# Half-contraction products of a GeGLU block: three stretches of them in place of four in the first and last block, and the array shape of the neighbouring attention product

## The chip, the cores and the metric

The kernel runs on one core of one Trainium2 chip. The metric is the device time of one execution in microseconds (us); a lower time is better. Engines are named as the profile names them: PE (TensorE, matrix products; PEld is its weight loading), DVE (VectorE), ACT (ScalarE), POOL (GpSimd), SP (SyncE, which here only issues transfers).

## The reference

The kernel computes a parallel transformer block on 2048 tokens of width 448, in bfloat16:

```python
xn = layernorm(x)                                  # x: 1 x 2048 x 448
q, k, v = split(xn @ wqkv)                         # 16 heads of width 28
s = where(0 <= i - j < 256, q @ k.T * 28 ** -0.5, -1e9)
attn = softmax(s) @ v @ wo
ffn = (gelu(xn @ w_gate) * (xn @ w_up)) @ w_down   # hidden width 1792, tanh gelu
out = x + attn + ffn
```

## The kernel before

**Blocks.** The tokens are worked through in four blocks of 512 columns (`QB`, `qb` 0 to 3). Each block has an attention stage and then a gate stage (`gated`, L412). During the attention stage of block n the planner (`Feed`, `share`) fills PE's time between score products with the down projection of block n-1, the q, k and v projections of block n+1 and, in block 0 and block 3, some of the up projections that the gate stage would otherwise do. After block 3 the last down projection stands alone.

**The gate stage.** The hidden width is 14 chunks of 128, taken as seven pairs f = 0, 2, ..., 12. The contraction is 448 = 3 x 128 + 64 long. So each 512-column result needs three full products (128 rows, `three`, by `mm3` at L228) and one half product (64 rows, `half`, by `mm_half` at L233). A half product uses only rows 0 to 63 or 64 to 127 of the array, so two of them, one from each side, go side by side. The last 64 rows of `w_gate` and `w_up` lie in the two sides of the tiles `wgu3` and `wug3` for that purpose. A pair f has two gate results in one tile `gt` of two accumulator banks, and two up results in single banks (`u`), unless its up half was done earlier (`early`: f = 2, 4, 8 in block 0, and 2, 4, 6, 8, 10 in block 3). An early pair holds its up results in `hT` in SBUF.

PE takes its instructions in the order in which they are written. A stretch of half products between full products is called an excursion here. L428 to L455 set it out: `dense` issues full products, `halves` half products, `end` issues the gelu on ACT (L452) and the multiplication with the up result on DVE (L454 for early pairs, L456 for others). The loop over `((0,), (2, 4), (6, 8), (10, 12))` gives four excursions in a block. Within a group of two, the first pair's full products come ahead of its halves and the second pair's full products come behind its halves, so that one excursion serves both:

```python
for fs in ((0,), (2, 4), (6, 8), (10, 12)):
    a = begin(fs[0]); dense(a, True)
    b = begin(fs[1]) if len(fs) > 1 else None
    halves(a, False)
    if b: halves(b, True)
    else: last_v()
    end(a)
    if b: dense(b, False); end(b)
```

(The quotation joins lines.) In pair 0's excursion, `last_v` puts the attention's last product with v, `pv(3)` (L552, products at L560), behind the halves. In blocks 1 to 3 these are 48 products, each on 64 rows and 32 columns of the array, in eight places; in block 0 they are 16 products on 128 rows and 32 columns. Their results are two banks `ov` (one in block 0). `add_halves` copies the first to `oc` on ACT (L548) and adds the second on DVE (L549); in block 0 one DVE copy does it (L570). In blocks 1 to 3, `pv(3)` issues this copy at once, so it stands ahead of pair 0's gelu in ACT's queue. `pv(2)`'s copy is held in the list `behind` until after the next exponential.

**Banks.** There are eight accumulator banks: two tiles of two banks for `gt` (pool `sps`, tag "s"), two single banks with tag "m" used in turn, and single banks "o" and "d". A new user of a bank waits for the engine that last read it.

**After each pair** comes `hook(f)`: the last steps of the softmax sums (`sums` at L534 to L537, `inverse` at L544, both on DVE, and `scale_o` on POOL, L527), and in blocks 0 and 1 also a normalisation of a later token tile (`norm`, L209, and in block 0 `stat`, L195 and L196, on DVE) and its transposition by a transfer that SP issues. For f = 4 it also issues the transfers of `collect`, for f = 10 those of `deliver`.

Of the kernel before, what the change touches and what calls it, by code (L numbers as in the profile page):

```python
# [16 lines left out]
P = 128  # L17
# [58 lines left out]
def kernel(  # L76
# [151 lines left out]
            nc.tensor.matmul(ps, lhsT=lhs(c), rhs=rhs(c), start=start and c == 0, stop=stop and c == 2,  # L228
                             skip_group_check=True)

    def mm_half(ps, lhs, rhs, hi, start, stop):
        p0 = 64 * hi
        nc.tensor.matmul(ps, lhsT=lhs[p0:p0 + 64], rhs=rhs[p0:p0 + 64], start=start, stop=stop,  # L233
                         tile_position=(p0, 0), skip_group_check=True)

    done = set()
    ring = [("m", "m", "d"), 0]
# [147 lines left out]
        hT = blk.tile([P, NF, QB], bf16, name="hT", tag="hT")  # L385
        hTs[qb] = hT

    def half(ps, f, gate, hi, ts, start, stop):

        w3 = wgu3 if gate != bool(hi) else wug3  # L390
        mm_half(ps, w3[:, f * P:(f + 1) * P], xnT[:, 3, ts], hi, start, stop)

    def three(ps, f, gate, ts, start, stop):
        w = wg if gate else wu
# [17 lines left out]
    def gated(qb, early, last_v, hook):  # L412

        ts = slice(qb * QB, (qb + 1) * QB)
        hT = hTs[qb]
        turn = ["o" if down_tag[0] == "d" else "d", down_tag[0]] * 4

        def begin(f):
            last_tag[0] = turn[0] if f not in early else last_tag[0]
            pr = dict(f=f, gt=phase[0].pool.tile([P, 2, QB], f32, name="gt", tag="s"), us=[])  # L420
            if f not in early:
                alone = (turn.pop(0), 1)
                tags = (("m", 2), alone)
                if qb == 0 and f == 0:
                    nxt = [ring[0][(ring[1] + i) % 3] for i in range(2)]
                    tags = [(x, 2 if x == "m" else 1) for x in nxt]
                    if "d" in nxt:
                        turn.insert(0, "o")  # L428
                for tag, n in tags:
                    pr["us"].append(psum.tile([P, QB], f32, name="u0", tag=tag, bufs=n))  # L430
            return pr

        def dense(pr, start):
            f = pr["f"]
            gs = [(pr["gt"][:, i, :], f + i, True) for i in range(2)]
            us = [(u[:, :], f + i, False) for i, u in enumerate(pr["us"])]
# [3 lines left out]
        def halves(pr, start):  # L440
            f = pr["f"]
            for i in range(2):
                if pr["us"]:
                    half(pr["gt"][:, i, :], f + i, True, 0, ts, start, not start)
                    half(pr["us"][i][:, :], f + i, False, 1, ts, start, not start)
                else:
                    half(pr["gt"][:, i, :], f + i, True, i, ts, start, not start)

        def end(pr):
            f = pr["f"]  # L450
            ge = work.tile([P, 2, QB], bf16, name="ge", bufs=2)
            nc.scalar.activation(out=ge[:, :, :], in_=pr["gt"][:, :, :], func=ACT.Gelu_apprx_tanh)  # L452
# [68 lines left out]
    def attention(qb, feeds, aux, plan):  # L521
# [25 lines left out]
        def add_halves(oc, ov):  # L547
            nc.scalar.copy(out=oc[:, :], in_=ov[0][:, :])  # L548
            nc.vector.tensor_tensor(out=oc[:, :], in0=oc[:, :], in1=ov[1][:, :], op=ALU.add)  # L549

        def pv(g):

            tags = ("o",) if not qb else ("m", "m" if g < 3 else down_tag[0])
            ov = [psum.tile([P, QB], f32, name="ov", tag=tag, bufs=2 if tag == "m" else 1) for tag in tags]
            todo = parts.pop(g)
            for n, (half, kt, q0, nq, col, p_sb) in enumerate(todo):
                k0 = 64 * half if half else 0
                r = slice(k0, k0 + (P if half is None else 64))
                for j in range(4):
                    nc.tensor.matmul(ov[half or 0][32 * j:32 * j + 32, q0:q0 + nq], lhsT=v_sb[r, kt, 4 * g + j, :],  # L560
                                     rhs=p_sb[r, j, col:col + nq], start=n == (half or 0), stop=n + len(tags) >= len(todo),
                                     tile_position=(k0, 32 * j), skip_group_check=True)
# [14 lines left out]
        for i, (scores, ncol, edges) in enumerate(steps):  # L577
            while (qb, scores[-1][0]) not in done:
                feeds[0].run()
            for fd in feeds:  # L580
                if fd.held:
                    fd.run()
            if i in pvs:
                pv(pvs[i])
            while fresh:
                apply_masks(*fresh.pop(0))
            if not qb and i - 1 in pvs:
                sums()
                inverse()
            if qb and i - 1 in pvs:  # L590
                sums()
            if qb and i - 2 in pvs:
                inverse()
            ss = phase[0].pool.tile([P, 4, QB], f32, name="sc", tag="s")
            p_sb = work.tile([P, 4, QB], bf16, name="p_sb", bufs=5)
            for g, half, kt, q0, nq, col in scores:
                k0, nk = (64 * half, 64) if half is not None else (0, P)
                for j in range(4):
                    r = slice(32 * j, 32 * j + Dh)
                    nc.tensor.matmul(ss[k0:k0 + nk, j, col:col + nq], lhsT=kT[r, g, kt * P + k0:kt * P + k0 + nk],  # L600
                                     rhs=qT[r, g, qb * QB + q0:qb * QB + q0 + nq], start=True, stop=True,
                                     tile_position=(32 * j, k0), skip_group_check=True)
                parts.setdefault(g, []).append((half, kt, q0, nq, col, p_sb))
            nc.scalar.activation(out=p_sb[:, :, 0:ncol], in_=ss[:, :, 0:ncol], func=ACT.Exp, scale=SCALE)  # L604
            while behind:
                add_halves(*behind.pop(0))
            if qb:
                fresh.append((p_sb, edges))
            else:
                for m in edges:  # L610
                    masked(p_sb, *m)
            while later:
                scale_o(*later.pop(0))
            left = len(steps) - i
            if left == 1:
                drain(feeds)
            elif not qb:
                share(feeds + [Feed()], 1e12, 0)
            else:
                to = plan.get(i, 0)  # L620
                whole = sum(f.left for f in feeds) + STEP * left + PV * sum(j > i for j in pvs)
                ahead = STEP + PV * (i + 1 in pvs) + (360 if to > 1000 else 0)
                late = 400 if i == 0 else 0
                want = (whole - late) / (left + 0.2) + late - ahead - to
                if i in pvs:
                    had = feeds[0].left
                    share(feeds[:1], min(1100, want), 0)
                    want -= had - feeds[0].left
                share(feeds, want, to)
            if aux:  # L630
                aux.pop(0)()
# [10 lines left out]
            elif copied:  # L642
                sums()

        return rest, after


    def pads(eng, dst, gs):
# [92 lines left out]
    for qb in range(NB):  # L741
# [29 lines left out]
        rest, after = attention(qb, feeds, aux, plan)  # L771
        nc.scalar.preload_act_table(ACT.Gelu_apprx_tanh)
        score_pool(2)
        if qb not in hTs:
# [13 lines left out]
                    if qb == 0:  # L788
                        stat(t + 6)

        gated(qb, early, rest, hook)
        if qb < NB - 1:
            nc.scalar.preload_act_table_set("natural_log_exp_and_others")

# [137 lines left out]
```

## Time and profile before

| what | value |
|---|---|
| median of three runs | 223.24 us (223.16 to 223.36) |
| the profiled execution | 223.5 us, its span 221.7 us |
| PE busy | 214.3 us, 97% of the span |
| DVE, ACT, POOL busy | 156.2 us (70%), 132.9 us (60%), 45.0 us (20%) |
| granted PE clock | full in all 40 slices |
| gate stages of blocks 0 to 3 | about 38.2 to 56.3, 85.3 to 107.9, 136.9 to 159.5 and 188.1 to 203.5 us |
| last down projection | from 203.3 us to the end |

Times inside an execution count from the start of the span. A row of the timeline gives the start, the duration, the engine and line, and how many instructions are merged. PE's products overlap: one of 512 columns shows a duration of 379 ns, but the next one starts 216 ns later, so PE's pace is read from starts, not from durations. PEld rows marked "issue" are loads that were not held up by any other engine.

### The profile page before, as it was taken

The page shows a single profiled execution, that of the slowest core. Times are in us where ns is not written, and L with a number is a line of the kernel's source. Part 1 is how long each engine was busy: PE and PEld are TensorE (multiplying, and loading weights), DVE is VectorE, ACT ScalarE, POOL GpSimd, SP SyncE. Part 2 cuts the span into 40 slices and gives each one's busy share as a digit, 9 for nine tenths or more (in the row PEclk, how much of TensorE's full clock was granted, in tenths as well). Part 3 has the DMA queues.
Part 4 walks back from the last instruction along what each step waited for, and adds up shares of the span by engine and source line. Part 5 has one row for each costly group of instructions (what it writes and reads, how often), then busy time and mean ns, then how long its engine had stood idle before and what let it go on. Part 6 is the DMA issues. An engine that isn't in the chain of part 4 may idle for free.

```text
span 221.7 us, 5352 instructions
## 1 busy us (share of the span) xinstructions
PE 214.3 (97%) x2240; PEld 94.9 (43%) x2240; DVE 156.2 (70%) x370; ACT 132.9 (60%) x129; POOL 45.0 (20%) x65
## 2 busy tenths in 40 slices
PE   6999999999999999999999999999999999999992
PEld 2433333344444444444444445444344435444571
DVE  5889996799666983679566896495444899479320
ACT  4497788644878875432878886233567778464000
POOL 5773687320000220022000031022000022022000
PEclk9999999999999999999999999999999999999999
DMA  6997699104200001102500000200000000000011
GB/s 193 304 296 94 174 326 305 22 1 74 44 3 21 24 24 29 18 3 44 70 1 23 24 1 26 57 5 0 0 4 21 24 3 24 21 0 4 22 43 25
DMA packets 18044, 13.28 MB, mean 60 GB/s; under 512 B 8704, under 2 KB 16992, under 8 KB 18016
## 3 DMA queue, kind: packets, MB, share of 16 engines
q1 hardware_dynamic: 17072, 12.62, 22.6%
q8 instruction: 18, 0.29, 0.6%
q10 hardware_dynamic: 944, 0.29, 0.5%
q14 instruction: 10, 0.08, 0.1%
HBM read 9.15 MB, written 2.18 MB: 51 GB/s over the span
## 4 chain that ended last, share of the span: by engine, by line
PE 95%; DVE 2%; ACT 1%; POOL 0%; issue 0%; DVEq 0%
PE po L375 20%; PE gt L228 17%; PE u L228 12%; PE sc L600 6%; PE po L370 6%; PE gt L233 5%; PE ue L228 5%; PE ov L560 5%; PE pq L228 4%; PE pv L228 4%; PE pk L228 3%; PE wps L190 2%; PE pq L233 2%; PE ue L233 1%; PE pv L233 1%; PE s L228 1%
## 5 line engine op out<-in xcount | busy, mean ns | idle before, releaser
L604 ACT ACTIVATE p_sb<-sc 128x2048 bf16<-128x2048 f32 (+2 forms) x42 | 73.8, 1758 | 12.6 <-PE sc L600 7.3
L375 PE MATMUL po<-wd,hT 128*128 128x448 bf16 (+1 forms) x238 | 50.0, 342 | 0.0
L452 ACT ACTIVATE ge<-gt 128x1024 bf16<-128x1024 f32 x28 | 28.7, 1025 | 33.6 <-PE u L233 20.9
L527 POOL TENSOR_TENSOR oN<-oc,l 128x512 bf16<-128x512 f32 x12 | 16.0, 1332 | 138.6 <-DVE l L544 88.2
L228 PE MATMUL gt<-xnT,wg 128*128 128x512 bf16 x168 | 40.3, 380 | 0.0
L456 DVE TENSOR_TENSOR hT<-ge,u 128x512 bf16<-128x512 bf16 x40 | 25.6, 682 | 9.7 <-ACT ge L452 9.6
L375 PEld LDWEIGHTS <-hT 128*128 128x128 bf16 x238 | 21.4, 98 | 18.6 <-issue 2.6
L228 PE MATMUL u<-xnT,wu 128*128 128x512 bf16 x120 | 29.2, 379 | 0.0
L508 DVE TENSOR_TENSOR p_sb<-p_sb,masks 128x256 bf16<-128x256 bf16 (+1 forms) x90 | 27.2, 357 | 0.4 <-ACT p_sb L604 0.4
L228 PEld LDWEIGHTS <-wg 128*128 128x128 bf16 x168 | 15.1, 98 | 21.4 <-issue 5.2
L228 PEld LDWEIGHTS <-wu 128*128 128x128 bf16 x168 | 16.0, 98 | 19.2 <-issue 1.0
L549 DVE TENSOR_TENSOR oc<-oc,ov 128x512 f32<-128x512 f32 x12 | 8.3, 688 | 18.3 <-ACT oc L548 18.3
L600 PE MATMUL sc<-qT,kT 28*64 28x320 bf16 (+7 forms) x640 | 16.9, 263 | 0.1
L380 DVE TENSOR_TENSOR res<-po,x_sb 128x448 bf16<-128x448 f32 (+1 forms) x17 | 10.0, 586 | 8.7 <-PE po L375 8.6
L370 PE MATMUL po<-wo,oN 128*128 128x448 bf16 (+1 forms) x68 | 15.9, 342 | 0.0
L518 POOL TENSOR_SCALAR_AFFINE_SELECT p_sb<-p_sb 128x512 bf16<-128x512 bf16 (+1 forms) x20 | 14.3, 736 | 7.8 <-ACT p_sb L604 7.6
L409 DVE CAST hT<-ue 128x512 bf16<-128x512 f32 x16 | 10.2, 680 | 6.3 <-PE ue L233 6.2
L548 ACT COPY oc<-ov 128x512 f32<-128x512 f32 x12 | 7.0, 584 | 11.9 <-PE ov L560 11.9
L233 PE MATMUL gt<-xnT,wgu 64*128 64x512 bf16 x48 | 13.2, 379 | 0.0
L228 PE MATMUL pq<-xnT,wqp 128*128 128x512 bf16 x45 | 12.2, 380 | 0.3 <-DVE v_sb L253 0.3
L534 DVE STREAM_TRANSPOSE l<-oc 128x512 f32<-128x512 f32 x16 | 11.3, 704 | 1.4 <-POOL oN L527 1.2
L228 PE MATMUL ue<-xnT,wu 128*128 128x512 bf16 x48 | 12.0, 380 | 0.0
(87 smaller groups left out, 236.0 us busy)
## 6 DMA issues: line engine op xcount, KB each, us to landing
out_dram<-res SPq DMA_DIRECT2D x15, 112.0 KB
x_sb<-in_A_x_dram SPq DMA_DIRECT2D x3, 448.0 KB
wu<-in_B_w_up_dram SPq DMA_DIRECT2D x1, 1344.0 KB
wg<-in_B_w_gate_dram SPq DMA_DIRECT2D x1, 1344.0 KB
wd<-in_B_w_down_dram SPq DMA_DIRECT2D x3, 448.0 KB
wraw<-in_A_wqkv_dram SPq DMA_DIRECT2D x2, 252.0 KB
wo<-in_A_wo_dram SPq DMA_DIRECT2D x4, 98.0 KB
wv<-in_A_wqkv_dram SPq DMA_DIRECT2D x1, 336.0 KB
```

Source lines behind the costliest of these rows:

```text
L228: nc.tensor.matmul(ps, lhsT=lhs(c), rhs=rhs(c), start=start and c == 0, stop=stop and c == 2, skip_group_check=True)
L233: nc.tensor.matmul(ps, lhsT=lhs[p0:p0 + 64], rhs=rhs[p0:p0 + 64], start=start, stop=stop, tile_position=(p0, 0), skip_group_check=True)
L370: nc.tensor.matmul(po[:, 0:w], lhsT=oN[:, g, cs], rhs=wo[:, g, lo:up], start=(g == 0), stop=False, skip_group_check=True)
L375: nc.tensor.matmul(po[:, 0:w], lhsT=hT[:, f, cs], rhs=wd[:, f, lo:up], start=False, stop=(f == NF - 1), skip_group_check=True)
L452: nc.scalar.activation(out=ge[:, :, :], in_=pr["gt"][:, :, :], func=ACT.Gelu_apprx_tanh)
L456: nc.vector.tensor_tensor(out=hT[:, f + i, :], in0=ge[:, i, :], in1=u[:, :], op=ALU.mult)
L508: nc.vector.tensor_tensor(out=reg, in0=reg, in1=m, op=ALU.mult)
L518: nc.gpsimd.affine_select(out=reg, in_=reg, pattern=mid + [[1 if diag else -1, min(w, P)]], compare_op=ALU.is_ge, fill=0.0, base=0 if diag ...
L527: nc.gpsimd.tensor_tensor(out=oN[:, g, :], in0=oc[:, :], in1=inv, op=ALU.mult)
L534: nc.vector.transpose(out=l1[:, :, :].rearrange("p a b -> p (a b)"), in_=oc[:, :])
L600: nc.tensor.matmul(ss[k0:k0 + nk, j, col:col + nq], lhsT=kT[r, g, kt * P + k0:kt * P + k0 + nk], rhs=qT[r, g, qb * QB + q0:qb * QB + q0 + ...
L604: nc.scalar.activation(out=p_sb[:, :, 0:ncol], in_=ss[:, :, 0:ncol], func=ACT.Exp, scale=SCALE)
```

## The change

Four things change.

1. In blocks 0 and 3 the groups of pairs are `(0, 2), (4, 8, 6), (10, 12)`: three excursions. The halves of pair 2 join those of pair 0 ahead of `pv(3)`, and a group of three has its first pair's full products ahead of the excursion and the full products of the other two behind it. Pair 8 comes before pair 6 in every queue. Blocks 1 and 2 keep four groups.
2. The middle pair of the group of three (f = 8, early in both blocks) has its two gate results in single banks ("m", and "o" or "d") in place of a `gt` tile, since three pairs are then open at once. Its gelu is two ACT instructions of 512 columns in place of one of 1024.
3. In blocks 1, 2 and 3 the halves of the group that holds pair 0 are issued as four products of 64 rows and 32 columns each (`m=32`), the shape of the `pv(3)` products behind them. In block 0 they stay 64 x 128.
4. In block 3, `pv(3)`'s copy goes to `behind`. The new `flush`, called behind each multiplication with an up bank, issues it: on ACT behind pair 0's gelu, on DVE between pair 0's two multiplications.

```diff
-    def mm_half(ps, lhs, rhs, hi, start, stop):
+    def mm_half(ps, lhs, rhs, hi, start, stop, m=P):
         p0 = 64 * hi
-        nc.tensor.matmul(ps, lhsT=lhs[p0:p0 + 64], rhs=rhs[p0:p0 + 64], start=start, stop=stop,
-                         tile_position=(p0, 0), skip_group_check=True)
+        for c in range(0, P, m):
+            nc.tensor.matmul(ps[c:c + m], lhsT=lhs[p0:p0 + 64, c:c + m], rhs=rhs[p0:p0 + 64], start=start, stop=stop,
+                             tile_position=(p0, c), skip_group_check=True)
...
+        def single(name, tag):
+            return psum.tile([P, QB], f32, name=name, tag=tag, bufs=2 if tag == "m" else 1)[:, :]
+
-        def begin(f):
+        def begin(f, apart=False):
             last_tag[0] = turn[0] if f not in early else last_tag[0]
-            pr = dict(f=f, gt=phase[0].pool.tile([P, 2, QB], f32, name="gt", tag="s"), us=[])
+            pr = dict(f=f, us=[])
+            if apart:
+                pr["gs"] = [single("g0", tag) for tag in ("m", turn.pop(0))]
+                return pr
+            pr["gt"] = phase[0].pool.tile([P, 2, QB], f32, name="gt", tag="s")
+            pr["gs"] = [pr["gt"][:, i, :] for i in range(2)]
...
         def end(pr):
             f = pr["f"]
             ge = work.tile([P, 2, QB], bf16, name="ge", bufs=2)
-            nc.scalar.activation(out=ge[:, :, :], in_=pr["gt"][:, :, :], func=ACT.Gelu_apprx_tanh)
+            if "gt" in pr:
+                nc.scalar.activation(out=ge[:, :, :], in_=pr["gt"][:, :, :], func=ACT.Gelu_apprx_tanh)
+            else:
+                for i, g in enumerate(pr["gs"]):
+                    nc.scalar.activation(out=ge[:, i, :], in_=g, func=ACT.Gelu_apprx_tanh)
...
             for i, u in enumerate(pr["us"]):
-                nc.vector.tensor_tensor(out=hT[:, f + i, :], in0=ge[:, i, :], in1=u[:, :], op=ALU.mult)
+                nc.vector.tensor_tensor(out=hT[:, f + i, :], in0=ge[:, i, :], in1=u, op=ALU.mult)
+                flush()
             hook(f)
 
-        for fs in ((0,), (2, 4), (6, 8), (10, 12)):
-            a = begin(fs[0])
-            dense(a, True)
-            b = begin(fs[1]) if len(fs) > 1 else None
-            halves(a, False)
-            if b:
-                halves(b, True)
-            else:
+        for fs in ((0, 2), (4, 8, 6), (10, 12)) if qb in (0, 3) else ((0,), (2, 4), (6, 8), (10, 12)):
+            prs = [begin(fs[0])]
+            dense(prs[0], True)
+            prs += [begin(f, len(fs) == 3 and f == fs[1]) for f in fs[1:]]
+            for pr in prs:
+                halves(pr, pr is not prs[0], 32 if qb and not fs[0] else P)
+            if not fs[0]:
                 last_v()
-            end(a)
-            if b:
-                dense(b, False)
-                end(b)
+            end(prs[0])
+            for pr in prs[1:]:
+                dense(pr, False)
+                end(pr)
...
+        def flush():
+            while behind:
+                add_halves(*behind.pop(0))
...
             if qb:
-                if g == 2:
+                if g == 2 or qb == NB - 1 and g == 3:
                     behind.append((oc, ov))
                 else:
                     add_halves(oc, ov)
```

More of the change, by code (lines that the diff above doesn't have):

```diff
@@ L386, in new_hT, with half @@
         hTs[qb] = hT
-    def half(ps, f, gate, hi, ts, start, stop):
+    def half(ps, f, gate, hi, ts, start, stop, m=P):
         w3 = wgu3 if gate != bool(hi) else wug3
-        mm_half(ps, w3[:, f * P:(f + 1) * P], xnT[:, 3, ts], hi, start, stop)
+        mm_half(ps, w3[:, f * P:(f + 1) * P], xnT[:, 3, ts], hi, start, stop, m)
     def three(ps, f, gate, ts, start, stop):
@@ L410, in gen_up, with gated @@
             yield -360
-    def gated(qb, early, last_v, hook):
+    def gated(qb, early, last_v, flush, hook):
         ts = slice(qb * QB, (qb + 1) * QB)
@@ L434, in dense, with halves @@
             f = pr["f"]
-            gs = [(pr["gt"][:, i, :], f + i, True) for i in range(2)]
-            us = [(u[:, :], f + i, False) for i, u in enumerate(pr["us"])]
+            gs = [(g, f + i, True) for i, g in enumerate(pr["gs"])]
+            us = [(u, f + i, False) for i, u in enumerate(pr["us"])]
             for ps, fi, gate in (gs + us if f else us + gs):
                 three(ps, fi, gate, ts, start, not start)
-        def halves(pr, start):
+        def halves(pr, start, m):
             f = pr["f"]
@@ L443, in halves @@
                 if pr["us"]:
-                    half(pr["gt"][:, i, :], f + i, True, 0, ts, start, not start)
-                    half(pr["us"][i][:, :], f + i, False, 1, ts, start, not start)
+                    half(pr["gs"][i], f + i, True, 0, ts, start, not start, m)
+                    half(pr["us"][i], f + i, False, 1, ts, start, not start, m)
                 else:
-                    half(pr["gt"][:, i, :], f + i, True, i, ts, start, not start)
+                    half(pr["gs"][i], f + i, True, i, ts, start, not start, m)
         def end(pr):
@@ L604, in attention @@
             nc.scalar.activation(out=p_sb[:, :, 0:ncol], in_=ss[:, :, 0:ncol], func=ACT.Exp, scale=SCALE)
-            while behind:
-                add_halves(*behind.pop(0))
+            flush()
             if qb:
@@ L643, in after @@
                 sums()
-        return rest, after
+        return rest, after, flush
     def pads(eng, dst, gs):
@@ L770 @@
         score_pool(1)
-        rest, after = attention(qb, feeds, aux, plan)
+        rest, after, flush = attention(qb, feeds, aux, plan)
         nc.scalar.preload_act_table(ACT.Gelu_apprx_tanh)
@@ L789, in hook @@
                         stat(t + 6)
-        gated(qb, early, rest, hook)
+        gated(qb, early, rest, flush, hook)
         if qb < NB - 1:
```

11 lines of the change are left out of this document (4 added, 7 removed).

## The prediction, made before the changed kernel ran

> **What bounds the kernel now.** I read the page's busy shares first, then the chain that ended last, then PE's waits, and then the timeline of the gate stages.
>
> ```profile
> PE 214.3 (97%) x2240; PEld 94.9 (43%) x2240; DVE 156.2 (70%) x370; ACT 132.9 (60%) x129; POOL 45.0 (20%) x65
> PE 95%; DVE 2%; ACT 1%; POOL 0%; issue 0%; DVEq 0%
> ```
>
> The first line is busy time by engine, the second the chain by engine. The span is PE's: 95% of the chain is products. PE's own list of waits on other engines has three entries, 2.7 us in all, and lies ahead of the first gate stage. So a gain must shorten PE's stream itself, and a loss must open a wait in it. The timeline of block 3's gate stage shows where the stream is not at full pace.
>
> ```profile
> 190.68 0.39 PE L233 MATMUL gt<-xnT,wgu 64*128 64x512 bf16 x1
> 190.90 0.38 PE L233 MATMUL gt<-xnT,wgu 64*128 64x512 bf16 x1
> 191.21 0.59 PEld L560 LDWEIGHTS <-v_sb 64*32 64x32 bf16 x48 [0.42 <-issue]
> 191.21 0.74 PE L560 MATMUL ov<-p_sb,v_sb 64*32 64x256 bf16 x48
> 191.89 1.47 PE L228 MATMUL gt<-xnT,wg 128*128 128x512 bf16 x6
> 192.13 0.59 ACT L548 COPY oc<-ov 128x512 f32<-128x512 f32 x1 [2.91 <-PE ov L560]
> 192.61 2.13 ACT L452 ACTIVATE ge<-gt 128x1024 bf16<-128x1024 f32 x2
> 193.29 0.39 PE L233 MATMUL gt<-xnT,wgu 64*128 64x512 bf16 x1
> 193.69 0.37 PE L233 MATMUL gt<-xnT,wgu 64*128 64x512 bf16 x1
> 194.01 2.76 PE L228 MATMUL gt<-xnT,wg 128*128 128x512 bf16 x12
> 196.71 0.39 PE L233 MATMUL gt<-xnT,wgu 64*128 64x512 bf16 x1
> 196.94 0.38 PE L233 MATMUL gt<-xnT,wgu 64*128 64x512 bf16 x1
> 197.25 2.76 PE L228 MATMUL gt<-xnT,wg 128*128 128x512 bf16 x12
> ```
>
> Starts carry it. Twelve full products from 194.01 take until 196.71, 2.70 us; at the steady pace of 0.216 they need 2.59, so 0.11 is lost going into the halves. Two pairs of halves take 0.54 (196.71 to 197.25) where 2 x 0.216 = 0.43 is streaming: 0.11 lost going back. **An excursion costs 0.21 to 0.22 besides its work**, though no engine is waited for. From the halves at 190.68 to the attention product at 191.21 is 0.53, again 0.10 over streaming: **a change between two kinds of tiles costs 0.10 as well.** The excursion at 193.29 is the twin of that at 196.71 and takes 0.72, not 0.54: its second pair starts 0.40 after the first, in place of 0.23. Pair 4 needs the `gt` tile that pair 0's gelu reads, and that gelu ran at 192.61, behind the copy at 192.13, which waited for the attention product. **That is a stall of 0.18.**
>
> **The change part by part.**
>
> *Groups of three.* One excursion less in block 0 and one in block 3; the half products themselves stay. 2 x 0.21 = 0.42 gained, all on PE.
>
> *Halves in the attention product's shape.* One kind of change less at `pv(3)` in blocks 1, 2 and 3: 3 x 0.10 = 0.30. Added: 12 products and 12 loads each in blocks 1 and 2 (16 for 4) and 18 each in block 3 (24 for 6). Streaming is the same if eight places work at once: 16 x 512 columns in eight places are two steps of 0.216, what two pairs take now. The nearest row is the attention product itself, in the same shape, side by side in the same eight places: 48 products between 191.21 and 191.89, 0.68. By the groups by form it has 16 products of 320 columns and 8 each of 256, 192, 128 and 64: 10240 columns, 1280 per place, 0.54 at 0.216 per 512. With 0.10 for the change, 0.04 is left for six steps. Its 48 loads start within 0.59, 12 ns each, under the products; 16 need 0.20 under 0.43 of streaming. I take nothing for the added loads. The ends: 0.04 gained over three blocks if the ramp into a new shape also goes, and 0.10 lost per step of eight (8 loads x 12 ns) if each step's loads stood bare. There are seven steps (2, 2 and 3), so 0.70. The row shows them hidden, so I stay at nothing.
>
> The Trainium skill, "TensorE: Matmul & The Clock Gate", Part 3, "The mechanism", speaks against this: a weight load passes running products only where its row group differs, and four quarters of one half share a row group. By that rule the 0.70 is paid and the sum is a gain of 0.20. The attention product's 48 loads, also four to a row group, stay inside its 0.68 here, so the trace does not bear this out.
>
> *The copy behind the gelu in block 3.* Pair 0's gelu needs only pair 0's halves. In block 0, where no copy stands ahead of it, it starts at 41.60, 0.70 after its halves at 40.90. After the change it starts 0.70 behind the halves in block 3 too and ends 1.73 behind them. The halves of pairs 0 and 2 (0.65) and `pv(3)` (0.68) end 1.33 behind the same point; two sets of full products (2.59) follow before pair 4's halves, whose `gt` tile is needed already by pair 4's full products, 2.6 behind it: 0.9 to spare. The 0.18 goes. The copy (0.58) and the addition (0.69) end some 3.1 behind the halves; the banks that they free are next used by pair 8's halves, 4.2 behind. The addition delays the second multiplication and then `sums`, but these start earlier than before by about 0.5, since the gelu no longer waits. The last POOL product `oN` (201.42 to 203.04 now, for the projection that starts at 203.30 and needs it with its fourth product, at 203.86) keeps its 0.8.
>
> *Two gelus for pair 8.* About 0.15 more on ACT (a copy of 512 columns takes 0.58, a gelu of 1024 takes 1.02). ACT idles 0.6 to 2 us before each of these gelus; nothing on PE follows.
>
> *Pair 8 before pair 6, DVE in block 0.* Here DVE is the near thing. Now it runs almost without a gap from 42.63 to 49.58 (copy, pair 0, sums, pairs 2 and 4, normalisation, statistics). After the change pair 6's multiplications stand behind pair 8's (0.6), a normalisation (0.5) and a statistic (0.8): I get 51.4 to 52.7. They free the "m" and "d" banks of pair 12's up halves, which PE reaches 10.9 us behind pair 2's full products. Those start at 42.05 + 0.22 = 42.27, so at 53.1: 0.4 to spare. Pair 6's own banks are freed by pair 0's multiplications at 44.51 and wanted at 45.4. The `gt` tile of pair 2 is read by 44.8 and wanted by pair 6 at 45.4. All hidden, thinly. If the 0.4 is gone, PE waits microsecond for microsecond.
>
> *SP.* Transfers keep their number. The transposition of token tile 9 goes behind that of tile 10, issued at about 53.2 (now 51.5); its reader, the v projection of block 2, starts that tile at 58.45. `deliver` stays behind pair 10, where it is now (54.59).
>
> *Everything later.* ACT's and DVE's chains into the next attention stage hang on PE's last full products and move with them, so the gain of a block stays.
>
> Sum: block 0 0.21, blocks 1 and 2 0.10 each, block 3 0.21 + 0.10 + 0.18 = 0.49: 0.90. The profiled execution took 223.5, a span of 221.7 and 1.8 around it: the span becomes 220.8 and the execution 222.6. It stood 0.26 over the median of the three runs; against that median of 223.24 the forecast is **222.34**. What a measurement of this kernel can tell from no change is about 0.2%, 0.45 us, so this is a gain of two such steps.
>
> **The rivals.**
>
> *Bare loads.* Seven steps pay 0.10: 222.34 + 0.70 = 223.04, no measurable change. For it: those loads would be under 512-column products that no row has in this shape. Against: the 0.04 above.
>
> *Two passes (the slower side).* The quarter products read the same 64 rows of `xnT` four times at once, where the attention product reads four different head columns. If eight of them took two passes, each of the seven steps would cost 0.216 more: 1.51, so 223.85. It decides against the change from 1.35 on (0.90 plus 0.45), that is from 0.19 per step. Against it: starts of two halves on one tile of `xnT`, side by side, are one instant in the rows (193.29).
>
> *The switch stays.* If the 0.10 comes with any new user of the eight places, the 0.30 is not gained: 222.64. By the Trainium skill, "TensorEngine Tiling (Array Packing)", "Key Properties", only a change of mode drains the engine, and a change of tile does not. The sum is the same by that rule, and no row here has two unlike products in one shape back to back.
>
> *DVE late in block 0.* If pair 6's multiplications come 0.4 to 0.8 later than I worked out, PE waits up to 0.4 ahead of pair 12's up halves: up to 222.74.
>
> **How the numbers follow.** My sum 0.72, the switch stays 0.05, DVE late 0.05, bare loads 0.08, two passes 0.10. Faster by over 0.2% is the first three, 0.82; within 0.2% 0.08; slower 0.10. The range that holds 8 in 10 is these three: from 222.1, with the excursions at 0.22, 0.04 for the ramps and the 0.1 to 0.2 by which medians of a few runs lie apart, to 222.9, DVE late and the same spread.
>
> **What would show it.** Right: two excursions of 0.21 gone, 64*32 halves followed by `pv(3)` 0.43 (blocks 1, 2) or 0.65 (block 3) behind their first start, a gate stage of block 3 that is 0.49 shorter and one of block 0 that is 0.21 shorter, and PE's list of waits as it is. Wrong: steps of those halves over 0.22 apart; a PE wait on DVE at pair 12 in block 0; a gain in the gate stages that the next attention stage gives back.

## The result and the profile after

| | before | changed |
|---|---|---|
| median of six runs, us | 223.32 (223.16 to 223.52) | 222.42 (222.32 to 222.67) |
| profiled execution, its span, us | 223.5, 221.7 | 222.38, 220.7 |
| gate stage of block 0, us | 17.874 | 17.661 (-0.213) |
| gate stage of block 1 | 22.648 | 22.544 (-0.104) |
| gate stage of block 2 | 22.649 | 22.544 (-0.105) |
| gate stage of block 3 | 15.283 | 14.774 (-0.509) |
| attention stages of blocks 1, 2, 3 | 28.939, 28.941, 28.550 | 28.945, 28.946, 28.551 |
| last down projection | 13.890 | 13.890 |

The changed kernel takes 0.9961 of the time before (95% interval 0.9949 to 0.9973): 0.90 us faster. The stages are measured between starts of weight loads in the traces: a gate stage from the first load of pair 0's up product to the first load of `oN`. Their four differences sum to 0.93. Before the first gate stage the changed kernel's trace is 0.14 longer and behind the last product it is 0.23 shorter; neither belongs to the edit, and together with 0.93 they make the 1.0 between the spans. One kernel below, `three_all`, had executions of two kinds, five of 240.68 to 242.53 us and three slower ones of 247.00 to 247.07: its median and its ratio are of the five, its trace is of one of the three.

In the changed file the lines behind the edit are shifted: half products are at L234, gelus at L459 (and L462 for a single bank), multiplications at L464 and L466, `pv` products at L574, the copy and the addition of `add_halves` at L558 and L559, the down projection at L376. First the busy shares and the chain of the changed kernel.

```profile
PE 210.7 (95%) x2257; PEld 95.2 (43%) x2282; DVE 156.2 (71%) x370; ACT 133.3 (60%) x131; POOL 44.7 (20%) x65
PE 91%; DVE 4%; DMA 1%; issue 1%; ACT 0%
```

The bound is the same: PE's products, with the same DVE work beside them and 0.4 us more on ACT. Part of the fall from 214.3 to 210.7 on PE is not real: the trace holds 2282 loads but only 2257 products, and in each gap of a missing record PE looks idle. PE's list of waits on other engines has one new entry, 0.8 us for DVE ahead of the first gate stage, and none inside a gate stage. Next is the timeline around the first excursion of block 3 (start, duration, engine and line, operation, count, and in brackets the idle time ahead).

```profile
190.41 0.33 PEld L234 LDWEIGHTS <-wgu 64*32 64x32 bf16 x20 [0.42 <-issue]
190.41 0.40 PE L234 MATMUL gt<-xnT,wgu 64*32 64x512 bf16 x4
190.63 0.39 PE L234 MATMUL gt<-xnT,wgu 64*32 64x512 bf16 x4
190.85 0.39 PE L234 MATMUL gt<-xnT,wgu 64*32 64x512 bf16 x4
191.07 0.73 PE L574 MATMUL ov<-p_sb,v_sb 64*32 64x256 bf16 x48
191.13 1.02 ACT L459 ACTIVATE ge<-gt 128x1024 bf16<-128x1024 f32 x1 [2.18 <-PE gt L234]
192.05 0.58 ACT L558 COPY oc<-ov 128x512 f32<-128x512 f32 x1
194.43 0.39 PE L234 MATMUL gt<-xnT,wgu 64*128 64x512 bf16 x1
194.65 0.38 PE L234 MATMUL g<-xnT,wgu 64*128 64x512 bf16 x1
194.87 0.38 PE L234 MATMUL gt<-xnT,wgu 64*128 64x512 bf16 x1
```

The three steps of narrow halves start 0.22 apart, and so does `pv(3)` behind the last of them: 0.66 from 190.41 to 191.07, with no 0.10 on top. The first row is 20 of the 24 loads of these steps: they lie beside the products (190.41 to 190.74) and hold none of them up. The gelu starts 0.72 behind the halves' first start and the copy follows it. The group of three at 194.43 also goes at 0.22 a step, so the stall of 0.18 is gone.

### The profile page after: what moved, and what is told of

It reads as the page before. It is cut to its first block, busy times and chain, and to the rows that moved or that the text cites. A ratio compares the mean times of both kernels' runs of the same rounds, so it can differ in the third digit from the quotient of the medians.

```text
span 220.7 us, 5415 instructions
## 1 busy us (share of the span) xinstructions
PE 210.7 (95%) x2257; PEld 95.2 (43%) x2282; DVE 156.2 (71%) x370; ACT 133.3 (60%) x131; POOL 44.7 (20%) x65
## 4 chain that ended last, share of the span: by engine, by line
PE 91%; DVE 4%; DMA 1%; issue 1%; ACT 0%
PE po L376 20%; PE gt L228 15%; PE u L228 12%; PE sc L614 6%; PE po L371 6%; PE gt L234 5%; PE ue L228 5%; PE ov L574 5%; PE pq L228 4%; PE pv L228 4%; PE pk L228 3%; PE pq L234 2%; DVE st L195 2%; PE g L228 1%; DMA x_sb<-in_A_x_dram 1%
## 5 line engine op out<-in xcount | busy, mean ns | idle before, releaser
L376 PE MATMUL po<-wd,hT 128*128 128x448 bf16 (+1 forms) x238 | 50.0, 342 | 0.0
L459 ACT ACTIVATE ge<-gt 128x1024 bf16<-128x1024 f32 x26 | 26.6, 1024 | 34.9 <-PE u L234 20.1
L228 PE MATMUL gt<-xnT,wg 128*128 128x512 bf16 x149 | 36.1, 379 | 1.0 <-issue 1.0
L466 DVE TENSOR_TENSOR hT<-ge,u 128x512 bf16<-128x512 bf16 x40 | 25.7, 682 | 11.9 <-ACT ge L459 11.8
L376 PEld LDWEIGHTS <-hT 128*128 128x128 bf16 x238 | 21.4, 98 | 18.6 <-issue 2.6
L559 DVE TENSOR_TENSOR oc<-oc,ov 128x512 f32<-128x512 f32 x12 | 8.2, 687 | 15.2 <-ACT oc L558 15.2
L410 DVE CAST hT<-ue 128x512 bf16<-128x512 f32 x16 | 10.2, 680 | 6.3 <-PE ue L234 6.2
L234 PE MATMUL gt<-xnT,wgu 64*128 64x512 bf16 (+1 forms) x67 | 12.7, 380 | 0.0
L228 PE MATMUL pq<-xnT,wqp 128*128 128x512 bf16 x36 | 11.7, 380 | 0.7 <-DVE v_sb L254 0.3
L558 ACT COPY oc<-ov 128x512 f32<-128x512 f32 x12 | 7.0, 584 | 8.8 <-PE ov L574 8.8
```

What stands on the lines that cost most here:

```text
L234: nc.tensor.matmul(ps[c:c + m], lhsT=lhs[p0:p0 + 64, c:c + m], rhs=rhs[p0:p0 + 64], start=start, stop=stop, tile_position=(p0, c), skip_gr ...
L376: nc.tensor.matmul(po[:, 0:w], lhsT=hT[:, f, cs], rhs=wd[:, f, lo:up], start=False, stop=(f == NF - 1), skip_group_check=True)
```

## The experiments

Each was timed in five rounds beside the kernel before on the same chip. A ratio is to the kernel before, with its 95% interval. "Groups", "shape" and "copy" stand for items 1, 3 and 4 of the change; item 2 comes with item 1.

**The parts one by one.** `groups_only` has the groups of three, with wide halves (m = P) and the copy at once:

```diff
-                halves(pr, pr is not prs[0], 32 if qb and not fs[0] else P)
+                halves(pr, pr is not prs[0], P)
...
-                if g == 2 or qb == NB - 1 and g == 3:
+                if g == 2:
```

> Only the groups of three pairs in blocks 0 and 3; halves 64 x 128 everywhere, and the last attention product's copy at once, ahead of pair 0's gelu. Switch theory (an excursion costs 0.21 us besides its work, a stall comes where a gelu is late for a bank): 0.42 gained for two excursions, but in block 3 the full products of pair 4 now come 1.3 us behind pair 2's, and the tile that they need is read by pair 0's gelu, which waits behind the copy: in that order the gelu ends about 0.6 after PE wants the tile, where the kernel before stalled for 0.18. So about 0.42 - 0.42 = 0.0 net: 223.3 us, no change, with a PE gap of about 0.6 between pairs 2 and 4 in block 3 and a gate stage of block 0 that is 0.21 shorter. Rival (the parts add up: fewer excursions give 0.42 by themselves): 222.9.

Measured: 223.02 (222.90 to 223.75), ratio 0.9995 (0.9987 to 1.0004): no change. The gate stage of block 0 is 0.213 shorter, as in the changed kernel; that of block 3 is 0.094 longer than before. ACT and PE in block 3's gate stage of this kernel:

```profile
192.34 0.58 ACT L558 COPY oc<-ov 128x512 f32<-128x512 f32 x1 [3.13 <-PE ov L574]
192.83 1.95 ACT L459 ACTIVATE ge<-gt 128x1024 bf16<-128x1024 f32 x2
193.91 1.46 PE L228 MATMUL gt<-xnT,wg 128*128 128x512 bf16 x6 [0.34 <-ACT ge L459]
```

The gelu again stands behind the copy. The `gt` tile that it frees is now wanted by pair 4's full products, 1.98 behind the start of `pv(3)` (two more halves stand ahead of `pv(3)`, none behind pair 2's full products); in the kernel before, pair 4's halves wanted it 2.30 behind that start. So the stall grows by 0.32, from 0.18 to about 0.5 (the row calls 0.34 of it idle, since a product's row lasts longer than its step), and the 0.21 of the saved excursion is lost in it: 0.5 - 0.18 - 0.21 = 0.11 longer, against 0.094. So the parts do not simply add up: in block 3 the groups are worth nothing without the copy's move.

`copy_only` is the other half of that pair: the old four groups, wide halves, the copy behind the gelu.

```diff
-        for fs in ((0, 2), (4, 8, 6), (10, 12)) if qb in (0, 3) else ((0,), (2, 4), (6, 8), (10, 12)):
+        for fs in ((0,), (2, 4), (6, 8), (10, 12)):
...
-                halves(pr, pr is not prs[0], 32 if qb and not fs[0] else P)
+                halves(pr, pr is not prs[0], P)
```

> Only the attention product's copy behind pair 0's gelu in block 3; four groups, halves 64 x 128. Switch theory: the stall of 0.18 at pair 4's halves goes and nothing else moves: 223.14 us. Rival (the gain of the whole change is the earlier gelu, which frees banks for all that follows): 0.5 or more, 222.8 or less.

Measured: 223.02 (222.86 to 223.44), ratio 0.9989 (0.9981 to 0.9998). Block 3's gate stage is 0.193 shorter, the other stages are unchanged. In its timeline pair 4's excursion runs at the streaming pace, where it had 0.40 between its steps:

```profile
191.55 1.02 ACT L459 ACTIVATE ge<-gt 128x1024 bf16<-128x1024 f32 x1 [2.16 <-PE gt L234]
192.47 0.58 ACT L558 COPY oc<-ov 128x512 f32<-128x512 f32 x1
193.46 0.39 PE L234 MATMUL gt<-xnT,wgu 64*128 64x512 bf16 x1
193.69 0.38 PE L234 MATMUL gt<-xnT,wgu 64*128 64x512 bf16 x1
```

`no_copy` is the changed kernel with the copy at once:

```diff
-                if g == 2 or qb == NB - 1 and g == 3:
+                if g == 2:
```

> The changed kernel with the attention product's copy in block 3 at once again, ahead of pair 0's gelu. Switch theory: pair 4's full products wait about 0.6 us for that gelu, a stall that the group of three has made longer than the 0.18 of the kernel before: 222.42 + 0.58 = 223.0 us. Rival (the copy's place is worth what it cost before, 0.18): 222.6.

Measured: 222.78 (222.54 to 223.20), ratio 0.9982 (0.9973 to 0.9991). Block 3's gate stage is 0.496 longer than the changed kernel's, all others are the same. The PE row is that of `groups_only` over again:

```profile
191.99 0.58 ACT L558 COPY oc<-ov 128x512 f32<-128x512 f32 x1 [3.02 <-PE ov L574]
192.47 1.95 ACT L459 ACTIVATE ge<-gt 128x1024 bf16<-128x1024 f32 x2
193.56 1.46 PE L228 MATMUL gt<-xnT,wg 128*128 128x512 bf16 x6 [0.34 <-ACT ge L459]
```

The mechanism is as expected, the price 0.08 smaller. Of the 0.509 of block 3, 0.496 hangs on the copy's place once the groups are there.

**The shape of the halves.** `shape_only` has the narrow halves beside `pv(3)` alone:

```diff
-        for fs in ((0, 2), (4, 8, 6), (10, 12)) if qb in (0, 3) else ((0,), (2, 4), (6, 8), (10, 12)):
+        for fs in ((0,), (2, 4), (6, 8), (10, 12)):
...
-                if g == 2 or qb == NB - 1 and g == 3:
+                if g == 2:
```

> Only the 64 x 32 shape of pair 0's halves beside the attention product in blocks 1 to 3; four groups in every block, the copy at once. Switch theory: three changes of kind gone at 0.10 each, 0.31 gained: 223.0 us; halves to attention product 0.43 in place of 0.54 in blocks 1, 2 and 3, the stall of 0.18 in block 3 stays. Rival (weight loads of the same row group stand bare, 0.10 for each of six steps): 0.6 lost against 0.31 gained, 223.6.

Measured: 223.84 (223.13 to 224.30), ratio 1.0021 (1.0010 to 1.0032): slower, against an expected gain. Yet the gate stages of blocks 1, 2 and 3 are 0.104, 0.105 and 0.107 shorter, as expected. The loss lies behind the last product's load: 5.66 us to the end of the span, where the kernel before has 4.69. What that is comes below.

`cols64` gives the changed kernel's narrow halves a shape that `pv(3)` does not have, two products of 64 columns for four of 32:

```diff
-                halves(pr, pr is not prs[0], 32 if qb and not fs[0] else P)
+                halves(pr, pr is not prs[0], 64 if qb and not fs[0] else P)
```

> The changed kernel with pair 0's halves (and pair 2's in block 3) cut into two products of 64 rows and 64 columns in place of four of 64 x 32, so beside the attention product, but not in its shape. Switch theory: the change of kind to the attention product is back at 0.10 in blocks 1, 2 and 3: 222.42 + 0.31 = 222.73 us. Rival (cutting the columns is what makes halves cheap, or any cut avoids the switch): 222.4, as the changed kernel.

Measured: 222.70 (222.22 to 223.89), ratio 0.9977 (0.9965 to 0.9988). The gate stages of blocks 1 to 3 are each 0.123 longer than in the changed kernel, in blocks 1 and 2 0.02 over those before. The timeline of block 1, first the changed kernel's, then that of `cols64`:

```profile
87.82 0.40 PE L234 MATMUL gt<-xnT,wgu 64*32 64x512 bf16 x4
88.05 0.39 PE L234 MATMUL gt<-xnT,wgu 64*32 64x512 bf16 x4
88.27 0.73 PE L574 MATMUL ov<-p_sb,v_sb 64*32 64x256 bf16 x48
```

```profile
87.78 0.40 PE L234 MATMUL gt<-xnT,wgu 64*64 64x512 bf16 x2
88.02 0.38 PE L234 MATMUL gt<-xnT,wgu 64*64 64x512 bf16 x2
88.33 0.74 PE L574 MATMUL ov<-p_sb,v_sb 64*32 64x256 bf16 x48
```

From the last halves to `pv(3)` it is 0.22 in the one, 0.31 in the other. The 0.10 is the price of a change of shape, not of a new user of the array: with the same shape on both sides, two quite unlike products follow each other at the streaming pace.

`cols32_all` goes the other way and cuts every half product of blocks 1 to 3 into four, so that all eleven excursions there pay the added loads, without a `pv` beside most of them:

```diff
-                halves(pr, pr is not prs[0], 32 if qb and not fs[0] else P)
+                halves(pr, pr is not prs[0], 32 if qb else P)
```

> The changed kernel with the halves of every excursion of blocks 1, 2 and 3 cut into 64 x 32 products, also where no attention product stands beside them (24 steps of eight products more in blocks 1 and 2 together, 6 in block 3). Switch theory: these excursions keep their two changes of kind, and loads are hidden; starts of eight products 3.3 ns apart in place of two make each change about 0.02 longer: 222.42 + 0.0 to 0.2. Rival (bare weight loads, 0.10 a step): 225.4. Rival (the narrow shape itself is cheaper): 0.10 gained for each of eight excursions, 221.6.

Measured: 222.41 (222.20 to 222.51), ratio 0.9961 (0.9947 to 0.9976), the same as the changed kernel. Its gate stages of blocks 1 to 3 are 0.051, 0.051 and 0.036 longer: 0.14 in all, 0.017 for each of the eight excursions that it alters. In one of them, in block 1, eight loads and eight products fill a step of 0.22:

```profile
91.72 0.40 PE L234 MATMUL gt<-xnT,wgu 64*32 64x512 bf16 x4
91.94 0.39 PE L234 MATMUL gt<-xnT,wgu 64*32 64x512 bf16 x4
```

So the added loads are hidden, and a narrow excursion between full products costs the same 0.2 as a wide one, but for that 0.017: there is nothing to gain by going narrow where no neighbour has that shape.

**DVE's spare time in block 0.** `dve_late` is the changed kernel with one statistic of a later token tile computed twice more behind pair 8, ahead of pair 6's multiplications in DVE's queue:

```diff
                     if qb == 0:
                         stat(t + 6)
+                        if f == 8:
+                            stat(t + 6)
+                            stat(t + 6)
```

> The changed kernel with DVE's statistic of token tile 14 computed three times in block 0, so that 1.5 us more stand ahead of pair 6's multiplications on DVE. In the changed kernel's timeline these end at 52.75, and PE reaches the bank that the second one frees at 53.31. Theory of the 0.4 to 0.6 us to spare: PE waits 0.9 to 1.0 us ahead of pair 12's up halves, and the time is 222.42 + 0.95 = 223.4. Rival (DVE is not near PE's path there): 222.4.

Measured: 223.21 (223.08 to 223.46), ratio 1.0001 (0.9992 to 1.0011). The gate stage of block 0 is 0.941 longer, no other stage moves. The timelines, first of the changed kernel, then of `dve_late`:

```profile
51.49 1.26 DVE L466 TENSOR_TENSOR hT<-ge,u 128x512 bf16<-128x512 bf16 x2
53.31 0.38 PE L234 MATMUL u<-xnT,wgu 64*128 64x512 bf16 x1
```

```profile
53.01 1.26 DVE L466 TENSOR_TENSOR hT<-ge,u 128x512 bf16<-128x512 bf16 x2
53.16 0.38 PE L234 MATMUL gt<-xnT,wgu 64*128 64x512 bf16 x1
53.73 0.37 PE L234 MATMUL u<-xnT,wgu 64*128 64x512 bf16 x1 [0.19 <-DVE hT L466]
54.33 0.37 PE L234 MATMUL u<-xnT,wgu 64*128 64x512 bf16 x1 [0.20 <-DVE hT L466]
```

Pair 6's multiplications move by 1.52 (51.49 to 53.01) and PE loses 0.94: DVE has 0.58 to spare here. The trace of the changed kernel says 0.56 directly: the multiplications end at 52.75, and pair 12's up halves start at 53.31. The view calls only 0.39 of the 0.94 idle, again because a product's row is longer than its step. By the starts all of it is the wait for the two multiplications: the first up half comes 0.57 behind the gate half that it should stand beside (53.73 and 53.16), and the second 0.60 behind the first in place of 0.22.

**The tail.** `shape_only` lost 1.0 us where no line of the edit works. In it the last addition of a result to `x` is late. The rows of DVE at the end, first before, then `shape_only`:

```profile
217.37 0.39 DVE L380 TENSOR_TENSOR res<-po,x_sb 128x224 bf16<-128x224 f32 x1 [1.33 <-PE po L375]
```

```profile
217.87 0.39 DVE L381 TENSOR_TENSOR res<-po,x_sb 128x224 bf16<-128x224 f32 x1 [1.89 <-DMA out_dram<-res]
```

It waits not for PE but for an earlier output transfer, since `res` has two buffers. And while the last output is written (218.2 to 220.5 in this trace), the view of the transfers lists one of PE's instruction transfers, 16 KB on queue q8, beside it:

```profile
q1 hardware_dynamic: 144, 0.06, 9.9%
q8 instruction: 1, 0.02, 3.4%
```

PE has 18 of these transfers before and 19 in the changed kernel and in `shape_only`; `cols32_all`, with 444 more products and loads than before, has 20; when the last of them comes depends on how many instructions PE has. My theory was that 72 more PE instructions (36 more products and their loads) move the last one into the output's way. Two kernels test it. `before_shift` has the four groups, the wide halves beside `pv(3)` and the copy of the kernel before, but cuts the halves of pairs 2, 4 and 6 of block 1 into four, which adds the same 72 instructions elsewhere:

```diff
-                halves(pr, pr is not prs[0], P)
+                halves(pr, pr is not prs[0], 32 if qb == 1 and pr["f"] in (2, 4, 6) else P)
```

> The kernel before with the halves of pairs 2, 4 and 6 of block 1 cut into 64 x 32 products, away from any attention product: 72 instructions more on PE, as many as the kernel with the shape alone has over the kernel before. Theory for that kernel's loss: its gate stages gained 0.32 us as expected, and 1.0 us was lost at the end of the span, where a 16 KB transfer of instructions, which comes once in 256 of PE's instructions, now falls on the write of the last output; how far PE's program is behind a multiple of 256 there is all that counts. Then this kernel, with the same 72 more, loses about 1.0 at the end too, and 0.03 in block 1: 223.25 + 1.0 = 224.2 us at its most frequent. Rival (the narrow shape beside the attention product costs something there that shows late): 223.3.

Measured: 224.25 (223.60 to 225.09), ratio 1.0045 (1.0029 to 1.0060). The time from the last product's load to the end is 6.20, 1.5 over that before; the gate stage of block 1 grows by only 0.14. `shape_shift` is `shape_only` with 48 more PE instructions, again in block 1:

```diff
-                halves(pr, pr is not prs[0], 32 if qb and not fs[0] else P)
+                halves(pr, pr is not prs[0], 32 if qb and not fs[0] or qb == 1 and pr["f"] in (2, 4) else P)
```

> The kernel with the shape alone (halves of pair 0 in blocks 1 to 3 in 64 x 32), and the halves of pairs 2 and 4 of block 1 cut in the same way: 48 more instructions on PE ahead of the last down projection, so that the transfers of instructions come some 4 us earlier against its outputs. Same theory: the 1.0 us at the end goes, 0.02 is lost in block 1, and the gain of the shape shows: 223.25 - 0.30 = 222.95 us. Rival (the shape itself costs it): 223.8.

Measured: 222.90 (222.73 to 223.19), ratio 0.9984 (0.9976 to 0.9993): a longer program that is 0.9 faster than `shape_only`, with a tail of 4.53. The last addition of `before_shift`, then that of `shape_shift`:

```profile
218.35 0.39 DVE L381 TENSOR_TENSOR res<-po,x_sb 128x224 bf16<-128x224 f32 x1 [2.12 <-DMA out_dram<-res]
```

```profile
217.34 0.39 DVE L381 TENSOR_TENSOR res<-po,x_sb 128x224 bf16<-128x224 f32 x1 [1.33 <-PE po L376]
```

All five kernels side by side, in us from the start of the last product:

| kernel | PE instructions over the kernel before | last two transfers on q8 start at | last output has landed at | last load to end of span |
|---|---|---|---|---|
| before | 0 | -15.65, -0.44 | 2.51 | 4.69 |
| `shape_only` | 72 | -1.37, 1.73 | 3.40 | 5.66 |
| `before_shift` | 72 | -1.12, 2.65 | 3.94 | 6.20 |
| changed | 84 | -2.93, 0.32 | 2.30 | 4.46 |
| `shape_shift` | 120 | -6.26, 0.15 | 2.36 | 4.53 |

That the length of PE's program decides, and not the shape of the halves, is shown by the two kernels: the loss comes without narrow halves beside `pv(3)` and goes with them kept. Six other traces, with 0, 28, 84 and 444 more PE instructions, have 4.34 to 4.66 in the last column.

The packet records in the traces show how, and that more than half of the loss comes from the second last transfer. In `shape_only` that one runs from -1.37 to -0.48, in `before_shift` from -1.12 to -0.24. Eight packets of the output that the late addition waits for start only then, at -0.49 and at -0.26; in the kernel before, that output is through by -1.20. So the addition starts at 0.85 and 1.09 in place of 0.30, and the last output is issued 0.55 and 0.79 later. The last transfer (1.73 to 2.99 and 2.65 to 3.53) then does the same to the last output: its last eight packets start at 2.98 and 3.52. In the kernel before, the transfer at -0.44 delays packets of the second last output in the same way, and nothing waits for that one. It was not tried with those transfers taken away.

How much is lost differs between executions. The traces are of the longest execution of each kernel (224.30 and 225.09). The shortest of `shape_only`, 223.13, is near the 222.93 that its gate stages alone would give (223.25 less 0.32). At the median, both kernels lose 0.9.

**Groups of three in blocks 1 and 2 too.** This was a try for a better version. A group of three needs an early middle pair, so `three_all` makes the up results of pairs 2, 4 and 8 of blocks 1 and 2 during their attention stages, and moves their `pv(3)` copies behind the gelu as well:

```diff
+                new_hT(qb)
+                early = (2, 4, 8)
-                feeds.append(Feed((gen_proj(qb + 1), PROJ)))
+                feeds.append(Feed((gen_proj(qb + 1), PROJ), (gen_up(qb, early), 3 * UP1)))
...
-        for fs in ((0, 2), (4, 8, 6), (10, 12)) if qb in (0, 3) else ((0,), (2, 4), (6, 8), (10, 12)):
+        for fs in ((0, 2), (4, 8, 6), (10, 12)):
...
-                if g == 2 or qb == NB - 1 and g == 3:
+                if g >= 2:
```

> The changed kernel with three excursions in blocks 1 and 2 as well: the up projections of pairs 2, 4 and 8 are done in the attention stage there too (behind the next block's projections), the groups are those of block 0, and the copy goes behind pair 0's gelu in blocks 1 to 3. Switch theory, if the attention stages take the moved products at PE's pace: 0.21 less in each of blocks 1 and 2, 222.42 - 0.42 = 222.0 us. Rival (DVE's six more copies of 0.68 us in each of these attention stages hold up the exponentials or the masks there): 222.8 or more, with PE waits in the attention stages of blocks 1 and 2.

Measured: 240.90 (240.68 to 242.53), ratio 1.0823 (1.0796 to 1.0850). In the trace, of an execution of 247.04, the attention stages of blocks 1 and 2 are 13.6 and 14.7 longer than in the changed kernel, their gate stages only 1.1 and 2.2 shorter. The up products pile up behind the last scores and wait there for the two "m" banks. Two rows of the timeline of block 1:

```profile
88.26 1.58 PE L228 MATMUL ue<-xnT,wu 128*128 128x512 bf16 x5 [2.57 <-ACT oc L558]
91.17 2.72 PE L228 MATMUL ue<-xnT,wu 128*128 128x512 bf16 x6 [0.78 <-DVE hT L410]
```

And the granted clock falls with these waits. The rows of stretches there give the stretch, its length, the busy time of PE, PEld, DVE, ACT and POOL with counts, the granted PE clock, the share of the transfers and GB/s:

```profile
88.00:90.00 2.00, 1.68 (x7) 0.58 (x7) 0.69 (x1) 1.50 (x2) 0.00 (x0) 0.90 0.20 34
90.00:92.00 2.00, 1.23 (x5) 0.38 (x4) 1.29 (x2) 0.00 (x0) 0.00 (x0) 0.50 0.00 0
100.00:102.00 2.00, 2.00 (x6) 0.73 (x5) 0.51 (x2) 0.00 (x0) 0.00 (x0) 0.50 0.03 8
```

`three_all2` lets the planner spread the same products over more gaps of the stage:

```diff
-                plan = {0: 1140, 1: 1140, 2: 1300, 4: 1300, 6: 1300, 7: 870}
+                plan = {0: 1140, 1: 1140, 2: 1300, 3: 1300, 4: 1300, 5: 870, 6: 1300, 7: 1300, 8: 1300}
```

> Three excursions in blocks 1 and 2 as well, as in the run before it, where all of the added up projections stood behind the last scores of the attention stage, on two banks, with PE waiting 2.6 us for ACT and then 0.8 for DVE at each pair, and the granted clock at 0.50 for some 13 us. Here the planner's amounts are set so that the up projections go between the scores of the stage, one pair behind each of the seventh to ninth steps, as in block 3. Switch theory: attention stages 3.9 us longer and gate stages 4.1 shorter in blocks 1 and 2, 222.0 us. Rival (DVE's six more copies in each of these stages reach PE): PE waits there, clock or no clock, 222.6 or more.

Measured: 231.91 (230.83 to 234.04), ratio 1.0391 (1.0350 to 1.0433). The pile is smaller, but the attention stages are still 8.6 and 10.2 longer, the gate stages 3.8 and 4.7 shorter. PE's list of waits (in all, times, longest) has new entries ahead of the `pv` products, behind casts of the added up results and copies of the projections:

```profile
PE ov L574 <- DVE hT L410: 3.1, 4, 1.3
PE ov L574 <- ACT qT L281: 1.3, 2, 0.7
PE ov L574 <- ACT qT L295: 0.9, 2, 0.5
```

These are 5.3 of the 18.8 that the two attention stages grew by. The moved products were expected to take 3.9 in each stage, 7.8 of it; where the other 5.7 went was not taken further (in block 2's stage the granted clock was 0.50 for 3.4 us). My sum for this version had an error of its own that no plan mends: each early pair carries a half-product excursion of its own in the attention stage, so three excursions are added in a block for one that is saved.

## Why the prediction was right

The measured gain, 0.90, is the predicted sum, and its terms hold one by one.

*Excursions, 0.21 each.* Block 0 gained 0.213, alone (`groups_only`) and with the rest.

*The change of kind, 0.10 in each of three blocks.* Blocks 1 and 2 gained 0.104 and 0.105; `shape_only` gained 0.104, 0.105 and 0.107. The rival that the switch stays is out: `cols64` has the same users in another shape and pays it again. By the Trainium skill, "TensorEngine Tiling (Array Packing)", "Key Properties", a change of tiling mode drains the engine and a change of tile does not. The runs agree as far as the price goes, 0.22 from the halves to `pv(3)` in one shape and 0.31 from 64*64 to 64*32; that the 0.09 is a drain, none of them shows.

*Nothing for the added loads.* Bare loads and two passes are out by the steps of 0.22 in block 3, and by `cols32_all`, where eight more excursions with four times the loads cost 0.017 each. The Trainium skill, "TensorE: Matmul & The Clock Gate", Part 3, "The mechanism", says in one sentence that a load passes running products only where its row group differs, and in another that the background weight buffer allows it too. In block 3 the loads of the second step, of both row groups, start by 190.46, while the first step's products of the same row groups run until the second step starts at 190.63. So the measurement decides against the first sentence taken alone.

*Block 3, 0.21 + 0.10 + 0.18.* Predicted 0.49, measured 0.509; the stall alone is 0.193 (`copy_only`). The gelu was worked out to start 0.70 behind the halves and started 0.72 behind them.

*DVE in block 0.* I gave 0.4 to spare; it has 0.56 to 0.58. That DVE would be late was the right rival to keep: the spare time is real but small, and beyond it PE paid what DVE was late by.

*Everything later.* The attention stages of the changed kernel lie within 0.006 of those before, so nothing was given back.

*What the working missed.* Two things, neither of which changed the result. The terms were priced as if they were independent. In block 3 they are not: without the copy's move, the groups would have opened a stall of 0.5 and lost their 0.21. The text worked out when pair 4's tile is needed, but only for the case with the move. And no term stood for the length of PE's program. It added 84 instructions, 12 more than a length that was measured to cost 0.9 at the median; a loss of that size would have taken the whole gain, and the forecast with it. The agreement of the sum rests to that extent on where the last instruction transfer fell. The tail's 0.2 and the start's 0.14 between the two profiled executions also show that agreement to 0.01 in the medians is partly chance.

## What to carry to other kernels

Where PE is the bound and has no waits, look at the starts of its products for seams: here 0.10 us at each change of tile shape, which goes when neighbours are given one shape, even if that needs four times the instructions. Before an order is changed, ask which release each product then needs sooner: a copy in front of a gelu cost 0.19 with the old order and 0.50 with the new. When a small edit moves the end of the span and none of its own stages, shift the length of the program somewhere harmless and see whether the loss goes with it.

## What the runs showed that was not expected

- The end of the span depends on PE's instruction count: 4.5 to 4.7 us from the last product's load to the end in the kernel before and with 84 or 120 more instructions, 5.7 and 6.2 with 72 more, in the longest execution of each. Transfers of PE's instructions delay packets of the last outputs, and an output that the last addition waits for matters most.
- Products of unlike kinds, 64 x 512 halves and attention products of 64 to 320 columns, follow each other at the streaming pace where both use 64 rows by 32 columns, and 0.09 to 0.10 later where one uses 64 by 64 or 64 by 128.
- In the trace of `three_all`, a wait on PE of 2.57 us and further ones of 0.78, one about every 4 us, went with a granted clock of 0.50, still there 12 us after the first wait, in a stretch in which PE was busy all the time. Six full products from 91.17 took 2.64 there, until the halves at 93.81, where six take 1.30 at 0.216; so part of the 13.6 lost in that stage is the clock's, and how much was not separated.
